# Attention state by head: 64x64 products in place of 128x128 blocks that are half zeros

## The chip, the core and the metric

The kernel runs on one core of one Trainium2 chip. The metric is device time in microseconds of one execution. Five engines work side by side and meet only through semaphores: TensorE (PE in the profile, with its weight loads as PEld), VectorE (DVE), ScalarE (ACT), GpSimd (POOL), and SyncE (SP), which here issues nearly all DMAs. Products are written to PSUM, eight banks of 128 partitions by 512 float32 values; everything else is held in SBUF.

## What is computed

Decayed linear attention over 2 batches, 8 heads, 768 tokens and head size 64, then two feed-forward blocks (512 to 2048 to 512, and 512 to 1536 twice, multiplied, to 512). All inputs of the feed-forward blocks are float64 weights. The part that the change touches is the attention state of each head, a 64x64 matrix that is carried from block to block:

```
for b in range(nb):
    qb, kb, vb = (q[:, :, sl], k[:, :, sl], v[:, :, sl])
    intra = np.einsum('bhic,bhjc->bhij', qb, kb) * Dmask[None]
    intra = np.einsum('bhij,bhjd->bhid', intra, vb)
    inter = np.einsum('bhid,bhde->bhie', qb * lam_pow[None], kv_state)
    out[:, :, sl] = intra + inter
    kb_dec = kb * rev_pow[None]
    kv_state = lam_block[None, :, None, None] * kv_state + np.einsum('bhsd,bhse->bhde', kb_dec, vb)
```

## The kernel before

Attention goes by 12 chunks of 128 tokens, called c0 to c11 here; c0 to c5 are the first batch and c6 to c11 the second, and a batch begins with an empty state (so c0 and c6 read no state, and c5 and c11 update none). Features lie on partitions: heads are kept in four pairs, head 2p on partitions 0 to 63 and head 2p+1 on 64 to 127. For each chunk the code makes:

- `att_scores`: scores of the 8 heads (L133), one product of 64 rows a head, even and odd heads into two PSUM banks;
- `att_mask`: `kd` = decayed keys (L145, POOL; DVE for c0), `pm` = masked scores (L154, two DVE operations), `qd` = decayed queries (L162, POOL; DVE for c3);
- `att_state`: the products of decayed keys and values (L174) into one bank `u`, and the state update. Three tiles `st` of [128, 4, 128] take turns. In each 128x128 block the two 64x64 blocks on the diagonal are the states of the pair's heads, and the other two are zeros, set once by POOL (L92). The product is made for the whole 128x128 block, and its two off-diagonal quarters are not used. The update takes the diagonal quarters one at a time: POOL multiplies the old state by the decay (L182), DVE adds the product (L186), or copies it at a batch's first chunk (L180);
- `att_out`: queries times state (L195, four products of 128 rows and 128 columns, with the zero blocks keeping the heads apart), then masked scores times values (L199, eight products of 64 columns, the two heads of a pair on the two partition halves of the same bank), summed in one bank. ACT then makes the rounded part of `x` (L211) and DVE the rest (L212).

All products of the attention are float32, and the trace shows two weight loads and two matmuls for each of them: 80 for the 40 products of L174, 192 for the 96 of L199.

Weights come as float64 bits. `split_w` rounds a [128, 512] tile to float32 and splits it in two parts, in four DVE operations (hc L253, v L257, L260 and L263), three on ACT (L252, L256, L284) and one on POOL (L285). The tiles are counted w0, w1, ... here. A feed-forward bank (`h_bank`) is 12 matmuls of 512 columns (L273) against `x` or `y` of 512 tokens, that is four chunks, followed by ACT (L292), DVE (L293, L294), ACT (L284) and POOL (L285).

The order of the work on PE and SP is the order in which the code is written (`manual_schedule`). DVE, ACT and POOL are ordered when the program is built, by a scheduler with costs of its own. c0 to c3 are done first; c4 to c11 are done in half steps between the first feed-forward banks (`att_step`). The second block of 512 tokens (c4 to c7) is first needed by the fifth `h_bank`, and from then on the feed-forward products follow one another to the end.

Of the kernel before, what the change touches and what calls it, by code (L numbers as in the profile page):

```python
# [8 lines left out]
F32 = mybir.dt.float32  # L9
# [5 lines left out]
ALU = mybir.AluOpType  # L15

B, H, S, D = 2, 8, 768, 64
CH = 128
# [7 lines left out]
FF1 = 2048  # L26
FF2 = 1536
PITCH = 272
# The upper halves, read as float32, of float32's largest value and of half its least normal one in float64.
HIGH_MAX = struct.unpack("f", struct.pack("I", 0x47EFFFFF))[0]  # L30
HIGH_MIN = struct.unpack("f", struct.pack("I", 0x38000000))[0]


@with_exitstack
def retention_ffn_kernel(ctx: ExitStack, tc: tile.TileContext, lam, att, w1i, w1o, w2ab, w2o, out):
    """Decayed linear attention, then two feed-forward blocks, with the activations kept transposed
    ([features, tokens]) from the attention to the last product.

    A float32 operand of a large product is held as two float32r parts, hi = round(x) to 12
    significant bits and lo = x - hi (exact), and a product is hi*hi + hi*lo + lo*hi in PSUM.  # L40
    """
    nc = tc.nc
    const = ctx.enter_context(tc.tile_pool(name="const", bufs=1))
    dram = ctx.enter_context(tc.tile_pool(name="dram", bufs=1, space=bass.MemoryType.DRAM))
# [12 lines left out]
    def t2(name):  # L57
        return t2_p.tile([128, 512], F32, tag="t2", name=name)

# [1 line left out]
    lamp = const.tile([128, 1], F32, name="lamp")  # L61
    base = const.tile([128, 8], F32, name="base")
    exi = const.tile([128, 8], I32, name="exi")
# [3 lines left out]
    tabq = const.tile([128, H // 2, CH], F32, name="tabq")  # L67
    half = const.tile([128, 1], F32, name="half")
    idle = const.tile([128, 512], BF16, name="idle")
    st = [const.tile([128, H // 2, 128], F32, name=f"st{i}") for i in range(3)]  # L70
    rows = dram.tile([H, PITCH], F32, name="rows")
    rbase = rows[0:1, 0:1]

# [1 line left out]
        return bass.AP(tensor=rbase.tensor, offset=rbase.offset + offset, ap=ap)  # L75

    def powers():
        # partition 16 h + a, column b: lam[h] ** (8 a + b + 1)
        nc.sync.dma_start(out=lamp, in_=bass.AP(tensor=lam.tensor, offset=lam.offset, ap=[[1, H], [0, 16], [1, 1]]))
        nc.gpsimd.iota(exi, pattern=[[1, 8]], base=0, channel_multiplier=8)  # L80
        nc.vector.memset(base, 0.0)
        nc.vector.memset(zrow[:, 0:CH], 0.0)
        nc.vector.memset(zrow[:, CH:CH + 1], 1.0)
        nc.vector.memset(half, 0.5)
        nc.scalar.dma_start(out=rows[:, 0:CH + 1], in_=zrow)
        nc.vector.tensor_scalar(out=exi, in0=exi, scalar1=127, scalar2=None, op0=ALU.bitwise_and)
        nc.vector.tensor_copy(exf, exi)
        nc.vector.tensor_scalar(out=exf, in0=exf, scalar1=1.0, scalar2=None, op0=ALU.add)
        nc.vector.tensor_scalar(out=base, in0=base, scalar1=lamp, scalar2=None, op0=ALU.add)
        nc.gpsimd.tensor_tensor(out=base, in0=base, in1=exf, op=ALU.pow)  # L90
        for s in st:
            nc.gpsimd.memset(s, 0.0)  # L92

    def warm(n):
        """Products of zeros that keep TensorE's clock up while it waits for the first data."""
        ps = bank()
        for i in range(n):
            nc.tensor.matmul(out=ps, lhsT=idle[:, 0:128], rhs=idle, start=True, stop=True)
# [12 lines left out]
                in_=raw_ap(CH + 1 + e * PITCH, [[0, 64], [2 * PITCH, H // 2], [1, CH]]),  # L111
            )

# [1 line left out]
    xy = {}  # L115
    ck = {}
    sc = {}
# [2 lines left out]
    qd = {}  # L120
# [45 lines left out]
    def att_state(c):  # L166
        cc = c % CPB
        if cc == CPB - 1:
            return
        u = bank()  # L170
        k = kd.pop(c)
        for pr in range(H // 2):
            cols = slice(pr * 128, (pr + 1) * 128)
            nc.tensor.matmul(out=u[:, cols], lhsT=k[:, cols], rhs=ck[c][3][:, cols], start=True, stop=True)  # L174
        u4 = u.rearrange("p (a e) -> p a e", a=H // 2)
        old, new = st[cc % 3], st[(cc + 1) % 3]
        for e in range(2):
            r, f = slice(64 * e, 64 * e + 64), slice(64 * e, 64 * e + 64)
            if cc == 0:
                nc.vector.tensor_copy(new[r, :, f], u4[r, :, f])  # L180
            else:
                nc.gpsimd.tensor_tensor(  # L182
                    out=new[r, :, f], in0=old[r, :, f],
                    in1=tabq[r, :, CH - 1:CH].to_broadcast([64, H // 2, 64]), op=ALU.mult,
                )
                nc.vector.tensor_tensor(out=new[r, :, f], in0=new[r, :, f], in1=u4[r, :, f], op=ALU.add)  # L186

    def att_out(c):
        cc = c % CPB
        o = bank()  # L190
        s = st[cc % 3]
        pairs = [(pr, slice(pr * 128, (pr + 1) * 128)) for pr in range(H // 2)]
        if cc:
            for pr, cols in pairs:
                nc.tensor.matmul(out=o[:, cols], lhsT=s[:, pr, :], rhs=qd[c][:, cols], start=(pr == 0), stop=False)  # L195
        for pr, cols in pairs:
            for e in range(2):
                h = 2 * pr + e
                nc.tensor.matmul(  # L199
                    out=o[64 * e:64 * e + 64, cols],  # L200
                    lhsT=ck[c][3][:, h * D:(h + 1) * D],
                    rhs=pm[c][e][:, pr * CH:(pr + 1) * CH],
                    start=(cc == 0 and pr == 0),
                    stop=(pr == H // 2 - 1),
                )
        nb, t0 = c // 4, (c % 4) * CH
        if nb not in xy:
            xy[nb] = xy_p.tile([128, 2, KT, TB], F32R, tag="xy", name="x")
        o4 = o.rearrange("p (a i) -> p a i", a=KT)
        hi, lo = (xy[nb][:, i, :, t0:t0 + CH] for i in range(2))  # L210
        nc.scalar.copy(hi, o4)  # L211
        nc.vector.tensor_tensor(out=lo, in0=o4, in1=hi.bitcast(F32), op=ALU.subtract)  # L212
        for d in (ck, pm, qd):
            d.pop(c, None)

# [1 line left out]
    wt = {}  # L217
    order = []
    for g in range(FF1 // 512):
# [16 lines left out]
    def split_w():  # L236
        if nxt["split"] >= len(order):
            return
        key = order[nxt["split"]]
        nxt["split"] += 1  # L240
        if key not in raws:
            load_w()
        r = raws.pop(key).rearrange("p (c w) -> p c w", w=2)
        low, high = r[:, :, 0], r[:, :, 1]
        pool, tag = (win_p, "win") if key[0][1] == "i" else (wout_p, "wout")
        w = pool.tile([128, 2, 512], F32R, tag=tag, name=tag)
        # float32 bits: sign and top exponent bit, 7 exponent bits and 20 of the fraction, then 3 rounded ones.
        # The magnitude is held to float32's range first: below it the result is 0, above it the largest.
        hc = t2_p.tile([128, 512], I32, tag="t2", name="hc")
        v = t2_p.tile([128, 512], I32, tag="t2", name="v")  # L250
        c = t2_p.tile([128, 512], I32, tag="t2", name="c")
        nc.scalar.activation(out=hc.bitcast(F32), in_=high.bitcast(F32), func=ACTF.Abs)  # L252
        nc.vector.tensor_scalar(  # L253
            out=hc.bitcast(F32), in0=hc.bitcast(F32), scalar1=HIGH_MIN, scalar2=HIGH_MAX, op0=ALU.max, op1=ALU.min
        )
        nc.scalar.activation(out=c, in_=low.bitcast(U32), func=ACTF.Copy, scale=2.0**-29)  # L256
        nc.vector.tensor_scalar(  # L257
            out=v, in0=hc, scalar1=3, scalar2=0x3FFFFFFF, op0=ALU.logical_shift_left, op1=ALU.bitwise_and
        )
        nc.vector.scalar_tensor_tensor(  # L260
            out=v, in0=high, scalar=-0x40000000, in1=v, op0=ALU.bitwise_and, op1=ALU.bitwise_or
        )
        nc.vector.tensor_tensor(out=v, in0=v, in1=c, op=ALU.add)  # L263
        split_act(v.bitcast(F32), w[:, 0], w[:, 1])
        wt[key] = w
        load_w()

# [1 line left out]
    def mm3(ps, pairs):  # L269
        n = len(pairs)  # L270
        for i, (l, r) in enumerate(pairs):
# [1 line left out]
                nc.tensor.matmul(out=ps, lhsT=l[a], rhs=r[b], start=(i == 0 and j == 0), stop=(i == n - 1 and j == 2))  # L273

    def product_in(kind, ft, nb):
        """One [128 features, 512 tokens] bank of x @ w."""
        ps = bank()
        w, x = wt[kind, ft], xy[nb]
        mm3(ps, [([w[:, a, k * 128:(k + 1) * 128] for a in range(2)], [x[:, b, k, :] for b in range(2)])
                 for k in range(KT)])  # L280
        return ps
# [27 lines left out]
    acc = {}  # L309

    def gather(total, ps, first):
        """Sum of the groups' parts."""
        if first:
            total = acc_p.tile([128, 512], F32, tag="acc", name="acc")
            nc.scalar.copy(total, ps)
# [65 lines left out]
        split_w()  # L381
        load_chunk(5)

    # the other chunks' attention, in steps between the first feed-forward products
    att_scores(4)
    att_mask(4)
    queue = [(c, half_way) for c in range(4, NCHUNK) for half_way in range(2)]
# [14 lines left out]
                load_chunk(c + 2)  # L402

    def ahead(used):
        """Weights in tiles that are split before the group at `used` needs them."""
        while nxt["split"] < min(used, len(order)):
            split_w()

# [90 lines left out]
```

## Time and profile before

| | us |
|---|---|
| median of 3 runs (lowest, highest) | 637.29 (636.66, 637.46) |
| span of the profiled execution, first to last instruction | 635.7 |
| PE busy in it | 615.7 |
| DVE busy in it | 380.9 |
| POOL busy in it | 253.0 |
| ACT busy in it | 247.4 |

The span is 1.6 us shorter than the median of the runs, which also take in what lies around the first and the last instruction. Busy times are sums over stages that differ: from 100 us on PE hardly ever pauses and the others have room; before that the attention and the first weights keep DVE busy nearly all the time. A PE that shows as busy is not necessarily at its peak: the granted clock, given per stretch as a share of the full clock, is 1.0 or 0.5 here (2.4 or 1.2 GHz).

### The profile page before, as it was taken

To read this page: it belongs to the slowest core of one execution; us is meant where nothing else is said; L and a number is where in the kernel's file an instruction comes from. 1 tells how busy PE (TensorE), PEld (TensorE's weight loads), DVE (VectorE), ACT (ScalarE), POOL (GpSimd) and SP (SyncE) were. 2 spreads that over 40 slices of the span, in tenths; PEclk is the share of its full clock that TensorE was granted. 3 is DMA by queue.
4 is the path that set the end of the run, shared out by engine and by line. 5 is a ranking of instruction groups with operands and counts; after the bars stand their busy time and mean duration, and the time that the engine had idled before them with its cause. 6 is when DMAs were issued, how large, how long until landed. Compare 5 with 4: busy or idle time off the path is not lost.

```text
span 635.7 us, 7943 instructions
## 1 busy us (share of the span) xinstructions
PE 615.7 (97%) x3012; PEld 507.3 (80%) x3012; DVE 380.9 (60%) x568; ACT 247.4 (39%) x421; POOL 253.0 (40%) x207
## 2 busy tenths in 40 slices
PE   5898799999999999999999999999999999999998
PEld 2777588888888888888888888888888888888886
DVE  0799794746976797588764433455545555555323
ACT  0245243454543354435643544433333333333110
POOL 2657763433533444354665432222223333333210
PEclk9789799999999999999999999999999999999999
DMA  6968321111210121021102122111111111210013
GB/s 185 379 243 293 111 68 34 66 35 66 100 66 34 66 84 56 34 94 66 67 34 67 67 67 67 66 65 62 56 51 69 64 68 66 67 34 1 1 67 133
DMA packets 20503, 52.70 MB, mean 83 GB/s; under 512 B 2408, under 2 KB 4208, under 8 KB 20464
## 3 DMA queue, kind: packets, MB, share of 16 engines
q1 hardware_dynamic: 20448, 52.18, 23.8%
q8 instruction: 24, 0.39, 0.3%
q14 instruction: 15, 0.12, 0.1%
q10 hardware_dynamic: 16, 0.00, 0.0%
HBM read 49.02 MB, written 3.15 MB: 82 GB/s over the span
## 4 chain that ended last, share of the span: by engine, by line
PE 89%; DVE 4%; DMA 2%; POOL 2%; issue 1%; ACT 1%; SPq 0%; DVEq 0%; POOLq 0%; ACTq 0%
PE ps L273 86%; PE ps L199 1%; PE ps L195 1%; PE ps L174 1%; DMA dmask<-rows 1%; DVE v L263 1%; DVE v L260 1%; DMA lamp<-in_lam 1%; DVE hc L253 1%; DVE v L257 1%; DVE pm L154 0%; DMA rows<-base 0%; POOL qd L162 0%; POOL kd L145 0%; DVE x L212 0%
## 5 line engine op out<-in xcount | busy, mean ns | idle before, releaser
L273 PE MATMUL ps<-y,win 128*128 128x512 f32 x864 | 198.8, 389 | 0.0
L273 PEld LDWEIGHTS ps<-y,win 128*128 128x128 f32 x864 | 162.2, 188 | 33.7
L273 PE MATMUL ps<-x,win 128*128 128x512 f32 x576 | 137.1, 396 | 3.3 <-DVE pm L154 2.6
L273 PE MATMUL ps<-g,wout 128*128 128x512 f32 x576 | 132.6, 389 | 0.0
L273 PEld LDWEIGHTS ps<-x,win 128*128 128x128 f32 x576 | 109.0, 190 | 27.4 <-ACT x L211 2.8
L273 PEld LDWEIGHTS ps<-g,wout 128*128 128x128 f32 x576 | 108.0, 188 | 22.6 <-issue 0.2
L285 POOL TENSOR_TENSOR win<-v,win 128x512 fp32r<-128x512 f32 x40 | 52.2, 1304 | 151.7 <-ACT win L284 151.7
L285 POOL TENSOR_TENSOR g<-r,g 128x512 fp32r<-128x512 f32 x48 | 67.2, 1399 | 85.3 <-ACT g L284 59.8
L273 PE MATMUL ps<-wout,g 128*128 128x512 f32 (+1 forms) x438 | 100.8, 386 | 0.0
L253 DVE TENSOR_SCALAR hc<-hc 128x512 f32<-128x512 f32 x68 | 37.2, 548 | 101.7 <-ACT hc L252 101.4
L273 PEld LDWEIGHTS ps<-wout,g 128*128 128x128 f32 x438 | 81.5, 188 | 16.7
L317 DVE TENSOR_TENSOR acc<-acc,ps 128x512 f32<-128x512 f32 (+1 forms) x97 | 64.7, 678 | 47.2 <-PE ps L273 47.2
L285 POOL TENSOR_TENSOR wout<-v,wout 128x512 fp32r<-128x512 f32 x28 | 36.8, 1313 | 85.1 <-ACT wout L284 85.0
L260 DVE SCALAR_TENSOR_TENSOR v<-raw,v 128x512 int32<-128x512 int32 x68 | 67.4, 991 | 2.3
L293 DVE SCALAR_TENSOR_TENSOR r<-r 128x512 f32<-128x512 f32 x48 | 37.9, 789 | 50.1 <-ACT r L292 50.1
L263 DVE CUSTOM_DVE_ANT_0 v<-v,c 128x1024 uint16<-128x1024 uint16 x68 | 56.3, 828 | 6.0
L284 ACT CAST win<-v 128x512 fp32r<-128x512 f32 x40 | 24.9, 622 | 87.1 <-DVE v L263 87.1
L302 ACT COPY a<-ps 128x512 f32<-128x512 f32 x36 | 21.1, 587 | 95.0 <-PE ps L273 93.6
L285 POOL TENSOR_TENSOR g<-a,g 128x512 fp32r<-128x512 f32 x36 | 46.5, 1292 | 25.8 <-ACT g L284 25.8
L292 ACT ACTIVATE r<-ps,half 128x512 f32<-128x512 f32 x48 | 32.8, 683 | 46.9 <-PE ps L273 46.9
L257 DVE TENSOR_SCALAR v<-hc 128x512 int32<-128x512 int32 x68 | 43.9, 646 | 5.0 <-DVE hc L253 0.9
L252 ACT ACTIVATE hc<-raw 128x512 f32<-128x512 f32 x68 | 45.3, 666 | 0.9 <-DMA raw<-in_w1i 0.9
(46 smaller groups left out, 395.4 us busy)
## 6 DMA issues: line engine op xcount, KB each, us to landing
raw<-in_w2ab SPq DMA_DIRECT2D x24, 512.0 KB, 3.2
raw<-in_w1i SPq DMA_DIRECT2D x16, 512.0 KB, 3.3
raw<-in_w1o SPq DMA_DIRECT2D x16, 512.0 KB, 3.2
raw<-in_w2o SPq DMA_DIRECT2D x12, 512.0 KB, 3.3
qT<-in_att SPq DMA_DIRECT2D x12, 256.0 KB, 4.7
kT<-in_att SPq DMA_DIRECT2D x12, 256.0 KB, 4.5
kn<-in_att SPq DMA_DIRECT2D x12, 256.0 KB, 5.2
vn<-in_att SPq DMA_DIRECT2D x12, 256.0 KB, 5.1
```

The costliest lines, as they stand in the source:

```text
L252: nc.scalar.activation(out=hc.bitcast(F32), in_=high.bitcast(F32), func=ACTF.Abs)
L253: nc.vector.tensor_scalar(out=hc.bitcast(F32), in0=hc.bitcast(F32), scalar1=HIGH_MIN, scalar2=HIGH_MAX, op0=ALU.max, op1=ALU.min)
L257: nc.vector.tensor_scalar(out=v, in0=hc, scalar1=3, scalar2=0x3FFFFFFF, op0=ALU.logical_shift_left, op1=ALU.bitwise_and)
L260: nc.vector.scalar_tensor_tensor(out=v, in0=high, scalar=-0x40000000, in1=v, op0=ALU.bitwise_and, op1=ALU.bitwise_or)
L263: nc.vector.tensor_tensor(out=v, in0=v, in1=c, op=ALU.add)
L273: nc.tensor.matmul(out=ps, lhsT=l[a], rhs=r[b], start=(i == 0 and j == 0), stop=(i == n - 1 and j == 2))
L284: nc.scalar.copy(hi, src)
L285: nc.gpsimd.tensor_tensor(out=lo, in0=src, in1=hi.bitcast(F32), op=ALU.subtract)
L292: nc.scalar.activation(out=r, in_=ps, func=ACTF.Relu, scale=0.5, bias=half)
L293: nc.vector.scalar_tensor_tensor(out=r, in0=r, scalar=1.0, in1=r, op0=ALU.min, op1=ALU.mult)
L302: nc.scalar.copy(a, pa)
L317: nc.vector.tensor_tensor(out=total, in0=total, in1=ps, op=ALU.add)
```

## The change

The state tiles become [128, 4, 64]: head 2p+e keeps its 64x64 state on partitions 64e to 64e+63, without zero blocks, and the three memsets of zeros go. `att_state` makes one product of 64x64 a head (eight in place of four), the two heads of a pair on the two partition halves of the bank `u`. The state update is one operation over 128 partitions on each engine, in place of one for each half. `att_out` makes queries times state in eight products of 64 rows by 64 columns: the even head in one quarter of the array, the odd head in the quarter diagonal to it. Comments were also cut, so line numbers of the changed code differ by a few.

```
-    st = [const.tile([128, H // 2, 128], F32, name=f"st{i}") for i in range(3)]
+    st = [const.tile([128, H // 2, D], F32, name=f"st{i}") for i in range(3)]
...
-        for s in st:
-            nc.gpsimd.memset(s, 0.0)
...
-        for pr in range(H // 2):
-            cols = slice(pr * 128, (pr + 1) * 128)
-            nc.tensor.matmul(out=u[:, cols], lhsT=k[:, cols], rhs=ck[c][3][:, cols], start=True, stop=True)
-        u4 = u.rearrange("p (a e) -> p a e", a=H // 2)
+        for h in range(H):
+            p0, pr = 64 * (h % 2), h // 2
+            nc.tensor.matmul(
+                out=u[p0:p0 + 64, pr * D:(pr + 1) * D],
+                lhsT=k[:, h * D:(h + 1) * D],
+                rhs=ck[c][3][:, h * D:(h + 1) * D],
+                start=True,
+                stop=True,
+            )
+        u4 = u[:, 0:H // 2 * D].rearrange("p (a e) -> p a e", a=H // 2)
         old, new = st[cc % 3], st[(cc + 1) % 3]
-        for e in range(2):
-            r, f = slice(64 * e, 64 * e + 64), slice(64 * e, 64 * e + 64)
-            if cc == 0:
-                nc.vector.tensor_copy(new[r, :, f], u4[r, :, f])
-            else:
-                nc.gpsimd.tensor_tensor(
-                    out=new[r, :, f], in0=old[r, :, f],
-                    in1=tabq[r, :, CH - 1:CH].to_broadcast([64, H // 2, 64]), op=ALU.mult,
-                )
-                nc.vector.tensor_tensor(out=new[r, :, f], in0=new[r, :, f], in1=u4[r, :, f], op=ALU.add)
+        if cc == 0:
+            nc.vector.tensor_copy(new, u4)
+        else:
+            nc.gpsimd.tensor_tensor(
+                out=new, in0=old, in1=tabq[:, :, CH - 1:CH].to_broadcast([128, H // 2, D]), op=ALU.mult
+            )
+            nc.vector.tensor_tensor(out=new, in0=new, in1=u4, op=ALU.add)
...
             for pr, cols in pairs:
-                nc.tensor.matmul(out=o[:, cols], lhsT=s[:, pr, :], rhs=qd[c][:, cols], start=(pr == 0), stop=False)
+                for e in range(2):
+                    r = slice(64 * e, 64 * e + 64)
+                    nc.tensor.matmul(out=o[r, cols], lhsT=s[r, pr, :], rhs=qd[c][r, cols], start=(pr == 0), stop=False)
```

PE's instructions keep their places; only their number and shape change. This is the piece of PE's queue from the scores of c3 to the state's product into c2's output, first before, then changed (L133 is L131 in the changed code, L195 is L199, L199 is L203 and L174 is L173; the last number is that of float32 products).

```order
L133 MATMUL ps<-qT,kT 128x128 x8
L195 MATMUL ps<-qd,st_94 128x128 x4
L199 MATMUL ps<-pm,vn 64x128 x8
L174 MATMUL ps<-vn,kd 128x128 x4
L195 MATMUL ps<-qd,st_95 128x128 x4
```

```order
L131 MATMUL ps<-qT,kT 128x128 x8
L199 MATMUL ps<-qd,st_94 64x128 x8
L203 MATMUL ps<-pm,vn 64x128 x8
L173 MATMUL ps<-vn,kd 64x64 x8
L199 MATMUL ps<-qd,st_95 64x128 x8
```

Nothing moved here, but neighbours that had one shape (L174 and L195, 128x128) now have two.

On DVE the scheduler, with the new costs, puts c2's state addition further ahead. Its queue from c2's masked scores to c3's decayed queries, first before (L186 is the addition into c2's new state, st_93), then changed (L188):

```order
L154 TENSOR_TENSOR pm<-ps,dmask 128x512 x2
L253 TENSOR_SCALAR hc<-hc 128x512
L257 TENSOR_SCALAR v<-hc 128x512
L154 TENSOR_TENSOR pm<-ps,dmask 128x512
L212 TENSOR_TENSOR x<-ps,x 128x4x128
L186 TENSOR_TENSOR st_93<-st_93,ps 64x4x64 x2
L260 SCALAR_TENSOR_TENSOR v<-raw,v 128x512
L154 TENSOR_TENSOR pm<-ps,dmask 128x512
L263 ISA v<-v,c 128x1024
L162 TENSOR_TENSOR qd<-qT,tabq 128x512
```

```order
L152 TENSOR_TENSOR pm<-ps,dmask 128x512 x2
L257 TENSOR_SCALAR hc<-hc 128x512
L261 TENSOR_SCALAR v<-hc 128x512
L188 TENSOR_TENSOR st_93<-st_93,ps 128x256
L216 TENSOR_TENSOR x<-ps,x 128x4x128
L264 SCALAR_TENSOR_TENSOR v<-raw,v 128x512
L152 TENSOR_TENSOR pm<-ps,dmask 128x512
L267 ISA v<-v,c 128x1024
L152 TENSOR_TENSOR pm<-ps,dmask 128x512
L160 TENSOR_TENSOR qd<-qT,tabq 128x512
```

The addition moved past c3's first masked scores and c1's `x`, which now stand behind it.

On POOL the decayed queries of c4 and c5 move back by one place each. POOL's queue from c4's state multiplication (st_95 from st_94) to the first feed-forward part g, first before, then changed:

```order
L182 TENSOR_TENSOR st_95<-st_94,tabq 64x4x64 x2
L145 TENSOR_TENSOR kd<-kn,dmask 128x512
L162 TENSOR_TENSOR qd<-qT,tabq 128x512
L285 TENSOR_TENSOR win<-v,win 128x512 x3
L162 TENSOR_TENSOR qd<-qT,tabq 128x512
L285 TENSOR_TENSOR g<-r,g 128x512
```

```order
L185 TENSOR_TENSOR st_95<-st_94,tabq 128x256
L143 TENSOR_TENSOR kd<-kn,dmask 128x512
L289 TENSOR_TENSOR win<-v,win 128x512
L160 TENSOR_TENSOR qd<-qT,tabq 128x512
L289 TENSOR_TENSOR win<-v,win 128x512 x2
L289 TENSOR_TENSOR g<-r,g 128x512
L160 TENSOR_TENSOR qd<-qT,tabq 128x512
```

The queries of c4 now stand behind w1's last step, and those of c5 behind the first bank's g. From c6 on DVE's and POOL's queues keep their order up to neighbours that change places.

## Rows read from the trace of the kernel before

**Rows 1.** The page, busy time of each engine (share of the span, instructions).
```profile
PE 615.7 (97%) x3012; PEld 507.3 (80%) x3012; DVE 380.9 (60%) x568; ACT 247.4 (39%) x421; POOL 253.0 (40%) x207
```

**Rows 2.** Stretches: length; busy PE, PEld, DVE, ACT, POOL (count); clock, DMA share, GB/s.
```profile
15.70:22.50 6.80, 5.28 (x30) 4.75 (x31) 4.02 (x7) 0.58 (x1) 3.48 (x4) 0.50 1.05 352
...
32.90:36.10 3.20, 3.20 (x25) 2.65 (x23) 2.96 (x6) 0.10 (x1) 3.05 (x4) 0.50 0.26 102
36.30:70.20 33.90, 29.97 (x264) 24.43 (x262) 32.64 (x46) 15.36 (x27) 20.24 (x18) 1.00 0.79 271
70.40:77.10 6.70, 4.91 (x11) 3.54 (x12) 4.59 (x9) 0.97 (x2) 6.40 (x8) 0.50 0.09 35
...
100.00:634.00 534.00, 532.66 (x2356) 441.12 (x2354) 304.64 (x450) 214.33 (x365) 195.20 (x148) 1.00 0.17 60
```

**Rows 3.** PE's timeline: start, length, instruction [idle before, releaser], c0 to c3.
```profile
17.22 2.05 PE L174 MATMUL ps<-vn,kd 128*128 128x128 f32 x8 [5.94 <-DVE kd L145]
19.20 1.98 PE L199 MATMUL ps<-pm,vn 128*64 128x128 f32 x16
21.11 1.84 PE L174 MATMUL ps<-vn,kd 128*128 128x128 f32 x8
...
23.97 1.16 PE L195 MATMUL ps<-qd,st 128*128 128x128 f32 x8
25.06 1.09 PE L199 MATMUL ps<-pm,vn 128*64 128x128 f32 x16
26.08 1.16 PE L174 MATMUL ps<-vn,kd 128*128 128x128 f32 x8
...
32.42 1.76 PE L195 MATMUL ps<-qd,st 128*128 128x128 f32 x8 [1.70 <-DVE qd L162]
```

**Rows 4.** DVE's timeline, c0 to c4.
```profile
17.04 1.28 DVE L154 TENSOR_TENSOR pm<-ps,dmask 128x512 f32<-128x512 f32 x2
19.38 0.88 DVE L180 COPY st<-ps 64x256 f32<-64x256 f32 x2 [1.06 <-PE ps L174]
...
23.05 0.87 DVE L186 TENSOR_TENSOR st<-st,ps 64x256 f32<-64x256 f32 x2 [1.49 <-PE ps L174]
...
36.75 0.69 DVE L212 TENSOR_TENSOR x<-ps,x 128x512 fp32r<-128x512 f32 x1 [0.76 <-ACT x L211]
37.36 1.34 DVE L263 CUSTOM_DVE_ANT_0 v<-v,c 128x1024 uint16<-128x1024 uint16 x1
38.62 1.27 DVE L154 TENSOR_TENSOR pm<-ps,dmask 128x512 f32<-128x512 f32 x2
```

**Rows 5.** Groups of POOL up to 100 us: count, busy us, mean ns, idle before.
```profile
L162 POOL TENSOR_TENSOR qd<-qT,tabq 128x512 f32<-128x512 f32 x9 | 12.3, 1368 | 0.1
L182 POOL TENSOR_TENSOR st<-st,tabq 64x256 f32<-64x256 f32 x16 | 11.1, 692 | 4.4 <-DVE st L186 3.1 <-DVE st L180 0.7
```

**Rows 6.** PE's timeline, c4 to c10.
```profile
41.31 1.16 PE L174 MATMUL ps<-vn,kd 128*128 128x128 f32 x8
42.30 1.06 PE L195 MATMUL ps<-qd,st 128*128 128x128 f32 x8
...
50.17 1.16 PE L195 MATMUL ps<-qd,st 128*128 128x128 f32 x8 [1.76 <-POOL qd L162]
...
71.42 0.80 PE L273 MATMUL ps<-x,win 128*128 128x512 f32 x1 [2.58 <-DVE pm L154]
72.98 4.72 PE L273 MATMUL ps<-x,win 128*128 128x512 f32 x11 [0.77 <-DVE x L212]
...
81.56 3.01 PE L273 MATMUL ps<-x,win 128*128 128x512 f32 x12
...
88.31 1.16 PE L174 MATMUL ps<-vn,kd 128*128 128x128 f32 x8 [0.73 <-POOL kd L145]
```

**Rows 7.** Landing of kT's DMAs up to 45 us.
```profile
DMA to landing us min/median/max: 4.0/4.7/8.8
```

**Rows 8.** SP's queue: the issue of c4's kT.
```profile
20.78 0.33 SPq L126 DMA_DIRECT2D kT<-in_att  x1
```

## The prediction

> **What bounds the kernel now.** The page first: PE is busy for 615.7 of 635.7 us [rows 1], which says little, since a PE that waits for nothing later can only be helped where it waits or where its own work shrinks. So the stretches, cut where the granted clock changes [rows 2]. From 100 us on PE is busy for 532.7 of 534 us and no instruction of the change is left. Everything is decided before. From 36.3 to 70.2 DVE is busy for 32.64 of 33.9 us, PE for 29.97: DVE is the bound, and PE waits for it. In the first chunks it is a chain that hops between engines: PE's state product, DVE's state addition, POOL's decays, PE again; DVE stands idle for 1.06 and 1.49 us for L174 and for 0.76 us for ACT's x, which follows c3's output [rows 4], while PE runs at half clock (0.50 from 15.7 to 22.5 [rows 2]). The chain of DVE ends at 72.9, when the last part of c7's x is made and the fifth feed-forward bank can go on at 72.98 [rows 6]. After that PE sets the pace, but for 0.73 us at 88.31 [rows 6]. So the prediction is: how much earlier comes 72.98, and what changes in PE's work between there and 100.
>
> **The prices.** *State product (L174, now 64x64).* Before, a burst is 8 full-array passes. Its duration is not its price; starts are: L195 at 23.97 to L199 at 25.06 is 1.09 us, of which about 0.1 is the change of shape, since L174 to L195 at 41.31 to 42.30, both full, is 0.99 [rows 3, 6]. That half-array products run two at a time is in the trace: L199's 16 passes of 64 columns of weights take 1.02 us, 25.06 to 26.08, where 8 full ones take 1.09 [rows 3]. The new burst is 16 passes as L199's, on the same partition halves of one bank, but with 64 columns streamed where L199 streams 128. No row has 64 columns. The bounds: no shorter than half of L199's streaming, so 0.6 us, no longer than L199, 1.02 us. I take 0.6, because the half clock doubles L199's burst (1.91 us, 19.20 to 21.11 [rows 3]): columns set the pace, not issue. At half clock: 1.05 (bounds 1.05 and 1.91) for the 2.05 of c0.
>
> *Queries times state (L195).* 8 full passes become 16 quarter passes of the same 128 columns. If the diagonal quarters run together, this is L199's 1.02 us against 0.99 to 1.09: nothing. Bounds: 0.1 less, or all 16 in series, 16 x 0.124 (0.99 for 8 without a change of shape) = 1.98, so 1.0 us more.
>
> *Changes of shape.* L174 and L195 had the shape of L273 and of one another; now they differ. c8, c9 and c10 have L273 ahead of L195, so 0.1 to 0.2 us each is added on PE where PE is the bound.
>
> *DVE's state step.* Two operations of 64x256 take 0.88 and 0.87 us; 512 elements a partition take 0.64 (1.28 for two [rows 4]) and 256 take 0.44. The time goes by elements of a partition, so one operation of 128x256 costs 0.44: 0.43 less for each of 10 updates. Bounds: 0 if it went by all elements; the rows exclude it.
>
> *POOL's state step.* Likewise 0.69 for 64x256 and 1.37 for 128x512 [rows 5]: 0.65 to 0.69 less for each of 8. The memsets run before anything waits for POOL: nothing.
>
> **The first part, up to 38.62, step by step.** c0's product ends at 18.3 and not 19.3. DVE's copy then goes at 18.35, right behind pm (which ends at 18.32 [rows 4]): the idle 1.06 is gone. c0's output runs 18.4 to 20.3 and c1's product to 21.3 (before: 21.11 plus 1.84). DVE, done with c1's pm at 20.1, still waits 1.3 for it. The addition ends at 21.85, where it ended at 23.92, and POOL's product, keys and queries for c2 follow as much earlier. PE is in c3's scores when the clock rises, at 22.5 if it rises as before, and ends c2's product at about 25.7. Here stands the added wait: c2's addition is now ahead of x, the weight steps and c3's masks on DVE; DVE reaches it at 25.5, so it holds all of these up for 0.25. DVE then works without a gap to qd of c3, done at about 30, where PE waited for it until 32.42 [rows 3]; PE's output of c3 ends at 32.2, or at 33.8 at half clock (1.76 and 1.91 us [rows 3]), and DVE comes to its x only at 34, so the idle 0.76 is covered either way. The sum on DVE: idle 3.31 before, 1.6 after, 1.7 gained; four state steps, 4 x 0.43 = 1.7; and L263, which took 1.34 beside POOL at 37.36 and 0.68 elsewhere, 0.3 of its 0.66 (bounds 0 and 0.66). Together 3.7 us earlier at the row 38.62.
>
> What could be late instead: loads. DMA is full in this stretch (share 1.05 [rows 2]). kT's slowest landing takes 8.8 us [rows 7]; c4's, issued at 20.78 [rows 8], is there by 29.6, and PE wants it at 32.2 now. That cover is 2.6 us; gone, each us costs one.
>
> **From 38.62 to 72.98** DVE works without a pause, so its saving counts whole: c4, c6 and c7, 3 x 0.43 = 1.3 us. PE saves three products there, which only lengthens its waits (1.76 at 50.17, 2.58 at 71.42 [rows 6]). POOL's moved step: c5's queries stand behind the first g, so L195 of c5 waits about 1.37 longer. Behind it on PE stand the next banks and c6, c7; DVE has their results to use only microseconds later, and PE's final wait of 2.58 covers it. Priced at 0; uncovered, 1.4.
>
> **After 72.98.** The keys of c10, which PE awaits at 88.31, hang on DVE's chain with c9's addition in it: 0.43 less. c10's product is 0.2 less after its change of shape; L195 of c8 and c10 0.2 more each, of which c8's lies in the same chain. About 0.3 less (bounds 0.9 less, 0.6 more).
>
> **Sum:** 3.7 + 1.3 + 0.3 = 5.3 us. The span of 635.7 becomes 630.4; the runs' median stood 1.6 above the span, so 637.3 becomes 632.0.
>
> **The rivals.**
>
> *Sixty-four columns are no faster, or the clock rises later* (633.9). If the new product costs L199's 1.02 (1.91 at half clock), DVE's idle hardly shrinks: the first part brings the four state steps and 0.3, 2.0 us; with 1.3 and 0.1, 3.4 in all. Against it: the doubling at half clock. A later rise gives the same: PE now has shorter bursts in the stretch at 0.50, and if this lasts another 3.2 us (the length of the second one [rows 2]), c3's scores, c1's output and c2's product end 1.9 later, and c2's addition holds DVE up. The Trainium skill (TensorE: Matmul & The Clock Gate, Part 1) says that without hardware decode a sequencer spends about 62 ns on each MATMUL, which then binds short ones. By that page the 16 passes would take an estimated 1.0 us at full clock; L199's average of 64 ns neither confirms nor excludes it.
>
> *The clock stays up at 70.4* (629.9). Eleven matmuls take 4.72 us there at half clock, twelve 3.01 at full [rows 6]; without the low stretch 2.0 more is gained. PE's wait, which precedes it, does not get shorter, so I give it little.
>
> *Diagonal quarters cannot run together* (641.0, slower). The even heads' rows and the odd heads' rows now write one bank. If PE takes them in turn, each burst of L195 is the 1.98 us from above, and eight hand-overs at the 0.1 of a change of shape make 2.8: 1.8 more than 1.02. c8 to c11 lie on PE's path: 7.2. c1 delays c2's addition: 1.5. c3 0.3; the others use up PE's waits. 9.0 more than forecast. It ends above 637.3 from 1.1 us more a burst on; series without hand-overs (1.0) gives 636.6. For it: L133, the only products of row halves in the trace, write two banks. Against it: L199's pairs write two partition halves of one bank, and do run together. The Trainium skill (TensorEngine Tiling (Array Packing), Gotcha 1: PSUM Pressure) says that different row tiles cannot access the same PSUM bank at once; it speaks for this rival, and no row here shows row tiles with different partitions in one bank.
>
> *Loads take over* (636.5, no change). If c4's loads or the next weights come as they did, DVE gets its work no earlier than before, and only c6's and c7's steps remain, 0.8.
>
> **How the numbers follow.** Chances: forecast 0.56; the first rival 0.19; clock up 0.05; loads 0.08; diagonal 0.12. What a measurement can tell from no change is 0.2%, 1.3 us. Faster has the first three, 0.80; same is loads, 0.08; slower is diagonal, 0.12. The range runs from the clock case with the bounds of L263, 629.4, to the loads case, 636.4; it leaves out the diagonal case and half of the loads, 0.16.
>
> **What would show it.** Right: L174's burst at 0.6 us from start to start, its c0 burst at about 1.05; L195's 16 passes in about 1.0; st on DVE at 0.44 x10; the pm of c4 near 34.9 and the fifth bank's second matmul near 68. Wrong: L195 at 1.8 or more; DVE idle for PE or ACT between 38 and 70; the first half-clock stretch past 22.6; PE waiting for kT of c4.

## The result, and the profile after

The changed kernel takes 630.16 us (median; 629.77 to 631.60) where the kernel before takes 637.38 (636.66 to 637.79): a ratio of 0.990, 95% interval 0.988 to 0.992, so 4.9 to 7.4 us faster. A second timing, beside the later experiments, gave 631.14 against 636.62, a ratio of 0.992 (0.990 to 0.993), 5.5 us by the medians where the first has 7.2; beside the experiments the kernel before had medians of 636.45 to 636.83, so its four runs here were on the long side. The forecast was 632.0, 5.3 us faster. Its sign and mechanism held. Of its three terms, 3.7, 1.3 and 0.3 us, these two profiles show 4.5, 1.0 and 1.2; the last was far too small, and the first leans on the state of one profile, as e4 shows below.

The page of the changed kernel, busy time of each engine with its share of the span of 628.0 us and its instructions [rows 1]:

```profile
PE 610.6 (97%) x3171; PEld 501.9 (80%) x3172; DVE 375.7 (60%) x558; ACT 247.6 (39%) x421; POOL 246.5 (39%) x196
```

Stretches of the changed kernel, cut where the granted clock changes; the columns are those of [rows 2]:

```profile
16.00:19.40 3.40, 3.14 (x41) 3.14 (x43) 2.97 (x6) 0.00 (x0) 1.95 (x3) 0.50 1.05 384
...
29.70:33.00 3.30, 3.30 (x29) 2.74 (x25) 3.13 (x4) 0.96 (x2) 1.51 (x2) 0.50 1.00 377
...
46.80:50.10 3.30, 3.30 (x26) 2.54 (x23) 3.16 (x5) 1.19 (x2) 1.19 (x2) 0.50 0.54 171
...
67.30:70.50 3.20, 3.20 (x9) 2.34 (x7) 1.62 (x3) 0.00 (x0) 2.67 (x5) 0.50 0.03 5
```

The half-clock stretches lie elsewhere than before, and those at the start and at the fifth bank are half as long (3.4 and 3.2 us, where [rows 2] has 6.8 and 6.7); the one at 46.8 is new. From 91.5 on nothing has changed: g's first matmul to the end takes 536.5 us in both kernels.

PE's timeline of the changed kernel, c0 to c5 (start, length, instruction, idle before it and releaser), to be held against [rows 3, 6]:

```profile
16.26 1.12 PE L173 MATMUL ps<-vn,kd 128*64 128x64 f32 x16 [5.04 <-DVE kd L143]
17.14 2.03 PE L203 MATMUL ps<-pm,vn 128*64 128x128 f32 x15
...
20.94 1.09 PE L199 MATMUL ps<-qd,st 64*64 64x128 f32 x16
21.96 1.09 PE L203 MATMUL ps<-pm,vn 128*64 128x128 f32 x16
...
37.06 0.69 PE L173 MATMUL ps<-vn,kd 128*64 128x64 f32 x16
37.67 1.09 PE L199 MATMUL ps<-qd,st 64*64 64x128 f32 x16
...
46.07 1.40 PE L199 MATMUL ps<-qd,st 64*64 64x128 f32 x16 [2.24 <-POOL qd L160]
```

Starts give the prices: the state product takes 0.61 us (37.06 to 37.67), at half clock 0.88 (16.26 to 17.14), and queries times state in quarters 1.02 (20.94 to 21.96).

DVE's timeline, c0 to c4 [rows 4]:

```profile
17.41 0.42 DVE L183 COPY st<-ps 128x256 f32<-128x256 f32 x1
17.76 1.28 DVE L152 TENSOR_TENSOR pm<-ps,dmask 128x512 f32<-128x512 f32 x2
20.02 0.42 DVE L188 TENSOR_TENSOR st<-st,ps 128x256 f32<-128x256 f32 x1 [0.99 <-PE ps L173]
20.36 0.68 DVE L216 TENSOR_TENSOR x<-ps,x 128x512 fp32r<-128x512 f32 x1
...
22.71 0.97 DVE L257 TENSOR_SCALAR hc<-hc 128x512 f32<-128x512 f32 x1 [0.47 <-ACT hc L256]
23.71 0.43 DVE L261 TENSOR_SCALAR v<-hc 128x512 int32<-128x512 int32 x1
...
33.11 1.28 DVE L152 TENSOR_TENSOR pm<-ps,dmask 128x512 f32<-128x512 f32 x2
```

The copy follows the masked scores without a wait, one wait of 0.99 us for PE is left where there were 1.06 and 1.49, and the 0.76 us for ACT's x is gone; a wait of 0.47 for ACT's hc is new. POOL's state step by group (count, busy us, mean ns, idle before) [rows 5]:

```profile
L185 POOL TENSOR_TENSOR st<-st,tabq 128x256 f32<-128x256 f32 x8 | 6.2, 771 | 2.2 <-DVE st L188 2.2
```

PE's timeline, c7 to g [rows 6]:

```profile
65.49 0.51 PE L277 MATMUL ps<-x,win 128*128 128x512 f32 x1 [1.78 <-ACT x L215]
66.48 4.38 PE L277 MATMUL ps<-x,win 128*128 128x512 f32 x11 [0.49 <-DVE x L216]
70.79 1.09 PE L199 MATMUL ps<-qd,st 64*64 64x128 f32 x16
...
73.93 0.69 PE L173 MATMUL ps<-vn,kd 128*64 128x64 f32 x16
74.54 3.01 PE L277 MATMUL ps<-x,win 128*128 128x512 f32 x12
...
80.88 0.69 PE L173 MATMUL ps<-vn,kd 128*64 128x64 f32 x16 [0.19 <-POOL kd L143]
...
91.49 11.18 PE L277 MATMUL ps<-g,wout 128*128 128x512 f32 x48
```

**Where the time went.** Four marks cut every profile into parts that can be held against one another, each a difference of two starts: *A*, from DVE's first kd to the masked scores of c4; *B*, from there to DVE's last x of c7; *C*, from there to g's first matmul. What lies ahead of A is the landing of loads; what lies behind C is constant. Times in us; the experiments follow below.

| kernel | median us | A | B | C | A+B+C |
|---|---|---|---|---|---|
| before | 637.38 | 22.19 | 33.61 | 26.94 | 82.74 |
| changed | 630.16 | 17.65 | 32.63 | 25.75 | 76.03 |
| changed, again | 631.14 | 17.64 | 32.64 | 25.73 | 76.01 |
| e1 state step split | 636.22 | 20.08 | 33.56 | 26.77 | 80.41 |
| e2 128 columns, c0 to c3 | 632.55 | 20.32 | 32.64 | 25.75 | 78.71 |
| e3 128 columns, c4 to c10 | 633.71 | 18.69 | 34.13 | 27.38 | 80.20 |
| e6 memsets back | 630.77 | 18.69 | 32.59 | 24.80 | 76.08 |
| e4 before, quarters | 637.28 | 20.30 | 34.00 | 27.15 | 81.45 |
| e5 before, narrow product | 636.26 | 20.04 | 33.85 | 27.52 | 81.41 |
| e9 first copy on ACT | 631.22 | 17.92 | 32.55 | 26.36 | 76.83 |
| e7 zero products first | 631.80 | 18.69 | 32.64 | 25.69 | 77.02 |
| e8 zero products before fifth bank | 630.10 | 18.69 | 32.60 | 24.84 | 76.13 |
| e11 decays early | 631.23 | 19.26 | 32.15 | 26.38 | 77.79 |
| e12 both | 631.18 | 19.55 | 32.12 | 25.29 | 76.96 |

Between the first two profiles 4.5 us come from A, 1.0 from B and 1.2 from C. That is one profile of the kernel before; e4, whose edit brings nothing, has an A of 20.30, and against it the three parts are 2.7, 1.4 and 1.4, 5.4 in all. The first profile also starts 0.97 earlier (DVE's kd at 15.46, before 16.43 [rows 4]), but the second profile of the same code starts at 16.29: that is the landing of a load, and no gain.

### The profile page after: what moved, and what is told of

It is laid out like the page before. It is cut to its first block, busy times and chain, and to the rows that moved or that the text cites. A ratio compares the mean times of both kernels' runs of the same rounds, so it can differ in the third digit from the quotient of the medians.

```text
span 628.0 us, 8231 instructions
## 1 busy us (share of the span) xinstructions
PE 610.6 (97%) x3171; PEld 501.9 (80%) x3172; DVE 375.7 (60%) x558; ACT 247.6 (39%) x421; POOL 246.5 (39%) x196
## 4 chain that ended last, share of the span: by engine, by line
PE 93%; DMA 3%; DVE 2%; POOL 1%; issue 1%; ACT 0%; SPq 0%; DVEq 0%; POOLq 0%
PE ps L277 89%; PE ps L203 2%; PE ps L199 1%; PE ps L131 1%; DMA raw<-in_w1i 1%; DMA tabq<-rows 1%; DMA lamp<-in_lam 1%; PE ps L173 1%; DMA rows<-base 0%; POOL base L90 0%; DVE pm L152 0%; DVE v L261 0%; POOL kd L143 0%; POOL qd L160 0%; DVE x L216 0%
## 5 line engine op out<-in xcount | busy, mean ns | idle before, releaser
L277 PEld LDWEIGHTS ps<-g,wout 128*128 128x128 f32 x576 | 108.1, 188 | 22.5 <-issue 0.2
```

## The experiments

The kernel before ran beside them at a median of 636.83 (e1, e2, e3, e6), 636.45 (e4, e5, e7, e9) and 636.62 (e8, e11, e12, the second timing).

**The state step in two halves again** (e1_split), all else as changed:

```
-        if cc == 0:
-            nc.vector.tensor_copy(new, u4)
-        ...
+        for e in range(2):
+            r = slice(64 * e, 64 * e + 64)
+            if cc == 0:
+                nc.vector.tensor_copy(new[r], u4[r])
+            ...
```

> The changed kernel with the state update in two halves of 64 partitions again, on POOL and on DVE; products as changed. Theory (DVE bounds 33 to 66 us, and every state step merged there or in the first chain counts whole): seven steps up to c7's x at 0.43 us and some of POOL's 0.65 in the first chain, 3.0 to 3.5 us lost, so about 633.4 against 630.2. Rival (what counted were PE's shorter products): 630.2 to 630.8.

Measured 636.22 us, a ratio of 0.999 (0.998 to 1.000): narrow products and quarters without the merged step bring next to nothing, and the loss, 5.1 to 6.1 us against the two timings of the changed kernel, is more than the 3.0 to 3.5 forecast. DVE's copy into c0's state, and the step behind it, in this kernel:

```profile
18.46 0.87 DVE L185 COPY st<-ps 64x256 f32<-64x256 f32 x2
19.36 1.29 DVE L152 TENSOR_TENSOR pm<-ps,dmask 128x512 f32<-128x512 f32 x2
```

From start to start the pair of halves holds DVE for 0.90 us; the merged copy above holds it for 0.35 (17.41 to 17.76). The step is worth 0.55, not the 0.43 that the durations gave, because instructions behind one another overlap by their ends and the pair did not gain by it. And the loss doesn't stay on DVE. PE's timeline of this kernel:

```profile
85.96 0.69 PE L173 MATMUL ps<-vn,kd 128*64 128x64 f32 x16 [2.44 <-POOL kd L143]
```

c10's keys, for which the changed kernel waits 0.19 us, are awaited for 2.44: POOL's own longer steps and DVE's reach PE where PE is the bound, and part C is 1.0 longer.

**The product with 128 columns, in c0 to c3 or in c4 to c10** (e2_wide_first, e3_wide_later); each head's 64 columns are streamed twice, and the second copy is not used:

```
+        wide = c < 4          # e3: c >= 4
...
+                    out=u[p0:p0 + 64, pr * 128:(pr + 1) * 128].rearrange("p (r e) -> p r e", r=2),
+                    rhs=v.rearrange("p (r e) -> p r e", r=1).to_broadcast([128, 2, D]),
```

> The changed kernel with 128 columns streamed for each head's state product (its 64 columns twice) in c0 to c3 alone; the results used are the same. Theory: in the first chain PE's product is what DVE waits for, at half clock, so c0 costs 0.8 and c1 0.4 to 0.8 more; 1.0 to 1.7 us lost, about 631.6. Rival (only DVE's and POOL's steps count): within 0.3 of 630.2.

> The same in c4 to c10 alone. Theory: the products of c4, c6, c7 and c8 lie in stretches where PE waits for DVE and cost nothing; c9's and c10's lie on PE's path, 0.4 each, of which c9's is partly in DVE's chain: 0.4 to 0.9 us lost, about 630.8. Rival (PE is the bound all along): 6 x 0.4 = 2.4, so 632.6.

e2 measured 632.55, a ratio of 0.994 (0.993 to 0.995): 1.8 us more than e6, which ran beside it, where 1.0 to 1.7 was forecast. B and C are those of the changed kernel to 0.01 us; all of the loss is in A. DVE's timeline there:

```profile
18.88 0.42 DVE L193 COPY st<-ps 128x256 f32<-128x256 f32 x1 [0.92 <-PE ps L176]
...
22.36 0.42 DVE L198 TENSOR_TENSOR st<-st,ps 128x256 f32<-128x256 f32 x1 [1.86 <-PE ps L176]
```

Both waits for PE are back. A narrow product is thus worth 1.6 us in the first chain against e6 and e8 (A of 18.69; in all three the first low stretch is 6.8 us long, and w0's steps lie beside POOL's, next point), and 2.7 against the changed kernel. No run has the merged step with 128 columns in every chunk, so what the merged step is worth without narrow products is not measured.

e3 measured 633.71, a ratio of 0.996 (0.994 to 0.997), more than the forecast of either theory for it. It doesn't settle what width costs later: the scheduler, with other costs, also put ACT's r of the third bank behind a weight step, DVE waited 1.28 us for that r, and the fifth bank ran all its eleven matmuls at half clock. PE's timeline:

```profile
69.16 5.06 PE L287 MATMUL ps<-x,win 128*128 128x512 f32 x11 [0.20 <-DVE x L226]
```

**The memsets back** (e6_memsets), on a tile that nothing reads:

```
+    zeros = const.tile([128, H // 2, 128], F32, name="zeros")
...
+        for _ in range(3):
+            nc.gpsimd.memset(zeros, 0.0)
```

> The changed kernel with three memsets of [128, 512] on POOL put back where they were (on a tile that nothing reads). In the profile after the change the decay table lands 0.9 us earlier, from DMAs that take less time each. Theory: that is the spread of the DMAs between executions, so 630.2 within 0.3. Rival: the memsets slowed the start, so about 631.1.

Measured 630.77, a ratio of 0.991 (0.990 to 0.993), within the two timings of the changed kernel: no cost shows. DVE's kd started at 16.64 here, and between 14.98 and 16.64 over all profiles, without relation to the edit. Its profile shows something else: A is 1.04 longer than in the changed kernel. e8 below, whose code up to there is the changed kernel's word for word, has the same 18.69, so it is not the edit. First DVE's timeline of e8, then POOL's:

```profile
20.67 0.42 DVE L188 TENSOR_TENSOR st<-st,ps 128x256 f32<-128x256 f32 x1 [1.30 <-PE ps L173]
...
22.81 1.52 DVE L257 TENSOR_SCALAR hc<-hc 128x512 f32<-128x512 f32 x1
24.36 1.16 DVE L261 TENSOR_SCALAR v<-hc 128x512 int32<-128x512 int32 x1
```

```profile
22.77 1.27 POOL L160 TENSOR_TENSOR qd<-qT,tabq 128x512 f32<-128x512 f32 x1
24.08 1.15 POOL L143 TENSOR_TENSOR kd<-kn,dmask 128x512 f32<-128x512 f32 x1
```

Each of the two DVE steps ends 0.29 us after the POOL step beside it (24.33 after 24.04, 25.52 after 25.23). In the changed kernel's profile POOL waited just then for a load, and v took 0.43 us. POOL's timeline there:

```profile
22.12 1.28 POOL L160 TENSOR_TENSOR qd<-qT,tabq 128x512 f32<-128x512 f32 x1
24.11 1.06 POOL L143 TENSOR_TENSOR kd<-kn,dmask 128x512 f32<-128x512 f32 x1 [0.72 <-DMA kn<-in_att]
```

The difference of 1.0 us is thus 0.3 of waiting for PE (1.30 and not 0.99, with PE at half clock for 6.8 us from 14.9 in e8), and 0.7 net from w0's first two steps: beside POOL they hold DVE for 2.63 us and not 1.35, of which 0.55 is made up, mostly because the changed kernel's profile has a wait of 0.47 ahead of them for ACT's hc, which itself waited for w0's load. The long low stretch is not needed for it: e3 has the same A of 18.69 with a first low stretch of 3.4 us. The Trainium skill (SBUF — State Buffer, Who interferes with whom) says that some DVE instructions and GpSimd's share a pair of ports as a lock, and that the later one waits until the other is done; these ends agree with it, though the 0.29 us left is less than the 0.42 of the step alone.

**One part alone in the kernel before** (e4_before_quarters, e5_before_narrow):

```
+                for e in range(2):          # e4, in att_out
+                    r = slice(64 * e, 64 * e + 64)
+                    nc.tensor.matmul(out=o[r, cols], lhsT=s[r, pr, r], rhs=qd[c][r, cols], start=(pr == 0), stop=False)
```

```
+        for h in range(H):                  # e5, in att_state
+            p0, hc = 64 * (h % 2), slice(h * D, (h + 1) * D)
+            nc.tensor.matmul(out=u[p0:p0 + 64, hc], lhsT=k[:, hc], rhs=ck[c][3][:, hc], start=True, stop=True)
```

> The kernel before, with queries times state alone made in quarters of 64 rows by 64 columns (the tiles keep their zero blocks and memsets, which are not read). Theory: the quarters run two at a time, so they bring nothing, and changes of shape at c8 to c10 cost 0.1 to 0.2 each: 637.4 plus 0.3 to 0.6. Rival (quarter products are part of the gain): below 637.0.

> The kernel before, with the state product alone made by head, 64 by 64, into the diagonal quarters of the bank; the update stays in two halves. Theory: the first chain gains what DVE idles for PE, about 1.5 us, and the last stretch 0.2: about 635.7. Rival (PE's product is most of the gain): 633 or less.

e4 measured 637.28, 1.0005 (0.9993 to 1.0018): the quarters bring nothing, as forecast. Its profile nevertheless has an A 1.9 us shorter than that of before. DVE's timeline of e4, then PE's, against [rows 3, 4]:

```profile
22.42 0.87 DVE L186 TENSOR_TENSOR st<-st,ps 64x256 f32<-64x256 f32 x2 [0.84 <-PE ps L174]
...
35.39 0.69 DVE L214 TENSOR_TENSOR x<-ps,x 128x512 fp32r<-128x512 f32 x1
```

```profile
21.12 1.20 PE L174 MATMUL ps<-vn,kd 128*128 128x128 f32 x8
...
31.79 1.09 PE L197 MATMUL ps<-qd,st 64*64 64x128 f32 x16 [1.77 <-DVE qd L162]
```

Up to c1's product PE has the same instructions in both kernels, and DVE's first kd starts at 16.44 here and at 16.43 before; but the first half-clock stretch lies from 14.4 to 21.2 in e4 and from 15.7 to 22.5 before, so that this product takes 1.20 us and not 1.84. c3's output runs at full clock in e4 and at half before. DVE then waits 0.84 us and not 1.49, and not at all for c3's x: of the 3.31 us of idle in [rows 4], 1.4 is not there in e4, and 0.65 of that lies ahead of the first instruction that the edit touches. It goes with where the low stretches fell in one profile of before. e4's runs lie in two groups, 635.65 to 636.21 and 637.27 to 637.95, and its profiled run is in the lower; the kernel before scatters over 635 to 638, and its profiled run was a long one.

e5 measured 636.26, 0.9992 (0.998 to 1.000), hardly more. Its A is 2.1 us below that of before's profile, but only 0.3 below e4's. Ahead of the two first state steps DVE waits 1.25 us less than in e4 (0.65 in all, against 1.06 and 0.84); 0.8 of that goes into the steps on w0 and w1, which take 7.05 us by starts where e4 has 6.23. Part C gives 0.4 back. PE's timeline of e5:

```profile
85.98 1.04 PE L174 MATMUL ps<-vn,kd 128*64 128x64 f32 x16 [2.52 <-POOL kd L145]
86.95 4.20 PE L273 MATMUL ps<-x,win 128*128 128x512 f32 x12
```

The keys of c10 are not ready, PE waits 2.52 us, and the bank behind that wait runs at half clock in part (4.20 us for what takes 3.01 in [rows 6]). Without the merged steps, DVE and POOL are late for c10 whatever the first chain gains, as in e1.

**What still bounds the first chain** (e9_copy_act, e7_warm_first): the first copy moved from DVE to ACT, and 24 products on zeros in place of 4 ahead of everything, so that PE is at full clock when c0 comes.

```
-            nc.vector.tensor_copy(new, u4)
+            nc.scalar.copy(new, u4)          # e9
```

```
-        warm(4)
+        warm(24)                             # e7
```

> The changed kernel with the copy of a batch's first state (c0, c6) on ACT in place of DVE. Theory (DVE bounds): c6's 0.43 us come off the bound, c0's only where DVE does not wait: 629.8. Rival (ACT's queue holds the copy up, and the state comes later): 630.2 to 630.8.

> The changed kernel with 24 products of zeros in place of 4 ahead of the first state product, so that PE works from 10.4 to about 15 us where it now waits for the decay table. Theory: the clock then stays at its upper level in c0 and c1, whose product, output and product take 2.1 us less, of which about 1.0 reaches the end, because DVE's first weight step then waits for its load: about 629.2. Rival (the loads bound the first chain): 630.2.

Neither helps: 631.22 (0.991) and 631.80 (0.992), the same as the changed kernel within the scatter of the runs, and above every forecast for the two. In e9, A became no shorter; B and C together grew by 0.5. In e7 the first state product ran at full clock, but the half clock only came later:

```profile
16.10:18.30 2.20, 0.90 (x18) 0.77 (x18) 1.69 (x3) 0.00 (x0) 0.00 (x0) 1.00 1.06 323
18.50:21.80 3.30, 3.25 (x34) 3.13 (x36) 1.84 (x4) 0.59 (x1) 2.82 (x3) 0.50 1.05 394
```

These are stretches of e7, columns as above. PE was at work for only 0.90 of 2.20 us ahead of the fall, for want of inputs. DVE in e7 still waited 1.46 us for c1's product and 0.75 for ACT's hc, which had waited 2.58 for w0's load: the loads have a part in what bounds the first chain.

**What bounds the last stretch** (e8_warm_fifth, e11_decay_early, e12_decay_warm): nine products on zeros ahead of the fifth bank, to keep the clock up; the decayed keys and queries of c5 to c11 made by POOL a step earlier; both.

```
+            if i == 1:
+                warm(9)                      # e8, e12
```

```
+                att_decay(c + 1)             # e11, e12, with the scores
```

> The changed kernel with nine products of zeros (1.9 us) on PE ahead of the fifth feed-forward bank, where PE waits for c7's x and the granted clock then falls to its lower level; the order on DVE, POOL and ACT is unchanged. Theory (the last stretch is bound by the chain through DVE and POOL to c10's keys): the bank runs 1.7 us faster at the upper level, but PE then waits longer for these keys; 0.5 to 0.9 us gained, about 629.5. Rival (PE's own work bounds the last stretch): the whole 1.7, about 628.5.

> The changed kernel with the decayed keys and queries of c5 to c11 written half a step earlier, with the scores: on POOL c5's queries then stand ahead of two weight steps and of the first g, and c10's keys ahead of a weight step; DVE's and ACT's orders are unchanged. Theory: PE's wait for c5's queries (2.2 us) goes, which DVE's bound hides, and the one for c10's keys (0.2 to 0.8) goes, which counts: 0.2 to 0.8 us gained, about 629.7. Rival (PE's waits around c5 count): 2 us or more, 628.2 or less.

> Both of the last two edits. Theory: with c10's keys early the fifth bank's faster run reaches the end: 1.7 for it and 0.2 to 0.8 for the keys, about 628.2. Rival (DVE bounds the last stretch whatever POOL's order): no better than the keys alone, 629.5.

e8 measured 630.10 (0.990, interval 0.988 to 0.992), 1.0 us below the changed kernel in the same company, but the intervals overlap. PE's timeline of e8:

```profile
67.44 3.18 PE L277 MATMUL ps<-x,win 128*128 128x512 f32 x12
...
81.29 0.69 PE L173 MATMUL ps<-vn,kd 128*64 128x64 f32 x16 [0.83 <-POOL kd L143]
```

The fifth bank runs at full clock, and 0.6 us of what that gives is spent again in the wait for c10's keys (0.83 instead of 0.19). That the products on zeros did it is not shown: e6, which has none, also ran this bank at full clock. In e11 those waits are gone, but PE then arrives at the fifth bank earlier, idles longer and runs all of it at half clock:

```profile
67.11 0.80 PE L285 MATMUL ps<-x,win 128*128 128x512 f32 x1 [3.61 <-ACT x L223]
68.11 5.06 PE L285 MATMUL ps<-x,win 128*128 128x512 f32 x11 [0.20 <-DVE x L224]
```

Its POOL steps also lie beside DVE's in the first chain (A is 1.6 longer): 631.23 (0.992), above both forecasts. In e12 the products on zeros waited for a bank themselves and then stood ahead of the fifth bank, whose x was ready at about 68.5 (DVE's step on it starts at 67.81 and takes 0.68):

```profile
66.41 0.59 PE L96 MATMUL ps<-idle 128*128 128x512 bf16 x1 [2.66 <-DVE r L306]
...
69.63 3.10 PE L285 MATMUL ps<-x,win 128*128 128x512 f32 x12
```

631.18 (0.991), again above both forecasts. No version beats the changed kernel by more than its own scatter.

**The changed kernel again** (after_again):

> The changed kernel itself once more, on the chip of the three others, to compare with. Theory: 630.2 within 0.8; and the time at which the decay table lands, 15.46 here once, spreads by about 1 us between executions as in the other runs (14.98 to 16.64), so that some of the difference of the two first profiles is chance. Rival: it lands at 15.5 again, so the change moved it.

631.14, 0.992 (0.990 to 0.993), with A, B and C equal to the first profile's within 0.02 us.

## Why the prediction was right, and where it was off

- **The state product** went as said: 0.61 us from start to start (0.6 said), 0.88 at half clock (1.05 said). The first rival, 64 columns no faster, is out by these rows; its other half, the later clock, by the first stretch, which ended earlier here (in e6 it ended at 23.2, past the 22.6 of the prediction, and the time was 630.77, not 633.9). The 62 ns per MATMUL of the Trainium skill (TensorE: Matmul & The Clock Gate, Part 1) do not bind in this trace: 16 passes in 0.61 us are 38 ns each.
- **Queries times state** went as said: 16 quarter passes in 1.02 us. The diagonal rival is out: 16 in series would have been 1.98. The Trainium skill (TensorEngine Tiling (Array Packing), Gotcha 1: PSUM Pressure) spoke for it; the measured 1.02 decides against that sentence for these quarters. The passes run in pairs that write the two partition halves of one bank, and e4 shows it in the time.
- **Changes of shape**: 0.2 us on PE, as said (81.50 to 86.49 is 4.99 us, with the queries of c10 and the output between two banks, where before 89.22 to 94.04 was 4.82).
- **The state step**: its duration went as said (0.42 on DVE; POOL 0.62 where nothing is beside it, 0.77 on average). The price was low: 0.55 a step by starts, where the durations gave 0.43. e1 shows that the merged step is the part without which the rest is worth next to nothing.
- **First part, 3.7 us forecast, 4.5 measured.** Idle: 1.46 us remained on DVE (0.99 for PE, 0.47 for ACT's hc) where 1.6 was said, in other places. State steps: 2.2, not 1.7. The 0.3 for L263 was the wrong item: what counts is the eight steps on w0 and w1 together, 6.71 us by starts before, 6.13 in the changed kernel's profile, and 7.23 in e6's. With POOL beside them, as in e6 and e8, A is 3.5 shorter; where POOL waits for a load, 4.5. That the forecast lies between is partly luck: it took the idle of 3.31 us from one profile, and in e4's the same waits are 1.90. Against e4, A is 1.6 to 2.7 shorter, most of it the four state steps (2.2), and the forecast is too high by 1.0 or more. The added wait of c2's addition (0.25 said) did not show. The rival of the loads did not decide: PE waited for no kT, though w0's load lies behind the 0.47 for hc.
- **38.62 to 72.98, 1.3 forecast, 1.0 measured**, and e1's B (33.56, like before's 33.61) shows that it is the merged step. By starts three steps are 1.7, and the masks and weight steps another 0.4. What takes back 1.1 is DVE's r, a step behind each bank: its first one lay beside a weight step of POOL, where before POOL was idle. DVE before, then DVE and POOL of the changed kernel:

```profile
45.61 0.68 DVE L293 SCALAR_TENSOR_TENSOR r<-r 128x512 f32<-128x512 f32 x1
```

```profile
38.98 1.77 DVE L297 SCALAR_TENSOR_TENSOR r<-r 128x512 f32<-128x512 f32 x1
```

```profile
38.73 1.47 POOL L289 TENSOR_TENSOR win<-v,win 128x512 fp32r<-128x512 f32 x1 [2.68 <-ACT win L288]
```

  c5's queries are awaited for 2.24 us, 0.48 more than before, not 1.37 more, and the wait was covered as said.
- **After 72.98, 0.3 forecast, 1.2 measured. This is the step that failed**: the term was mis-sized fourfold. The prediction had c10's keys come 0.43 us earlier for c9's merged addition, less up to 0.2 for c8's change of shape, and PE's own work behind them unchanged (0.2 less for the product, 0.2 more for shapes). Measured from DVE's last x of c7, the keys came 0.94 earlier (15.14 us to c10's product, before 16.08), and PE's work from there to g is 0.25 less (10.61, before 10.86). Of the 0.94, 0.35 was there when DVE took up the fifth bank's r (5.88 us after c7's x, before 6.23): this bank took 4.31 us by starts (66.48 to 70.79) where it took 4.56, with half the low stretch gone. The rest, 0.6, is about the merged addition's price by starts (0.55). PE could follow because its own work ahead of the keys shrank as well: c9's product takes 0.61 (73.93 to 74.54) and before 0.92. Two rows of PE before, behind the fifth bank:

```profile
77.54 1.05 PE L195 MATMUL ps<-qd,st 128*128 128x128 f32 x8
...
80.64 1.16 PE L174 MATMUL ps<-vn,kd 128*128 128x128 f32 x8
```

  So the clock, which the prediction left as it was and gave 0.05 to stay up, explains about a quarter of the shortfall of 0.9 directly (0.25). In e6 and e8, where it does stay up there, C is 24.8, 0.9 below the changed kernel; that rival had said 2.0, and the wait for c10's keys (0.8 and not 0.19) takes part of it. Why the clock falls in one profile and not in another of the same code at this place (e6 idles 1.79 and 0.48 us ahead of the bank, the changed kernel 1.78 and 0.49) stays open.
- **Start and memsets**: nothing that shows, as said (e6).

The errors add up: 0.8 in A, less 0.3 in B, 0.9 in C is 1.4 us, the distance from 5.3 to the 6.7 of the table. Against e4 (5.4) and by the second timing (5.5) the sum fits, but with A about 1 us too high and C about 1 too low: there the total is right by luck.

## What to carry to other kernels

A cut of work on one engine of a chain that hops between engines is worth what the next engine in the chain lets through: narrower products alone (e5) brought nothing clear of the noise, though DVE waited 1.25 us less in the first chain, and with the merged step beside them they are worth 1.6 there (e2). Take the idle that a sum starts from out of more than one profile: here 1.4 of 3.3 us came and went with the clock. Price a short instruction by the distance to the next start, not by its length. And where PE alternates between waiting and working, put a price on the granted clock in both states as a term of the sum, since profiles of the same code differ in it.

## What the runs showed that was not expected

- Two of DVE's steps between SBUF tiles, 0.42 us alone, took 1.16 to 1.52 when POOL's steps lay beside them, and ended 0.29 us after POOL's (e8). Some 0.7 us of A goes with whether a load makes POOL late.
- The low clock moves about: with 24 products on zeros (e7) the first low stretch began 1.9 us after DVE's first kd, in the changed kernel 0.5 us after it. The changed kernel has four low stretches of 3.2 to 3.4 us up to g; e6 and e8 have only the first, of 6.8. In e11 the one at the fifth bank is 6.8 us long, but in e9, which leaves the keys and queries as they are, it is too, so e11's shorter waits are not shown to be the reason.
- Profiles of nearly the same code differ by 1.0 us in A and 0.9 in C with opposite signs: A+B+C is 76.03, 76.01, 76.08 and 76.13 for the changed kernel (twice), e6 and e8.
